# Where a softmax sum gets its small constant, and how many routing scatters a step issues

## The chip, the core and the metric

The kernel runs on one core of a Trainium2 chip. The metric is the device time of one launch in microseconds (us), taken as the median of a few runs. The core has five engines with a queue of instructions each: TensorE (PE in the profile, with PEld for its weight loads), VectorE (DVE), ScalarE (ACT), GpSimd (POOL) and SyncE (SP), which here only issues DMAs. An engine takes its instructions in the order in which they stand in its queue. Waits between engines go over semaphores.

## The reference

Three stages follow each other, all in float32. Only what matters here is shown.

```python
# attention: batch 4, heads 8, sequence 576, head size 64
scores = scale * (q @ k.T)
kth = the 32nd largest score of the row
attn = exp(where(scores >= kth, scores, -1e9) - max)
attn = attn / (sum(attn) + 1e-09)
x = attn @ v                       # 2304 tokens x 512
# dense expert
h = x @ w_in;  x = (h * clip(h + 3, 0, 6) / 6) @ w_out
# routed experts: 8 of them, the two best for each token
noisy = x @ w_gate + log1p(exp(x @ w_noise)) * noise
out[token] += weight * (relu(x[token] @ w1[e]) @ w2[e])
```

The change touches the sum with its `1e-09` and the writing of the routing lists.

## The kernel before, in words

**Attention and the dense expert** are one pipelined loop in `phase_a`. The 2304 tokens are 18 tiles of 128, each with 8 heads, so there are 144 pieces of (tile, head), and step `st` of the loop works on several pieces in different stages: transposes of `q` and `k` for one, scores for the one before, then the search for the 32nd largest score (two steps on VectorE), exponentials (ScalarE), the product `y` that finds the threshold (GpSimd, `ysum`), the mask with the row's sum (VectorE, `pmask`), the transposes of the masked row and the product with `v`. Two heads make a pair, and a pair's two sums stand in one small tile, `SUM[p]`. In the first step after a pair's second `pmask` its reciprocal is made in three moves: `recip1` adds 1e-9 on GpSimd, `recip2` takes the reciprocal on VectorE, `recip3` spreads it over 64 columns on GpSimd (`rb`), from where it goes to TensorE and then scales the pair's output.

In the same steps, once two tiles are through (a "chunk"), one of 16 slices of the dense expert is worked on per step: `mm1` (tile `h`), a gate on VectorE (`hgate`, tile `r`), rounding on ScalarE, the low part on GpSimd (`hlow`, tile `g`), `mm2` (tile `xa`).

From step 22 on (`KEEP`) the four engines get the loop's instructions in just the order in which the loop emits them; every call goes through the wrapper class `Lane` at line 87, so nearly all instructions of this phase carry L87 in the profile. Before step 22, and for routing, a planner that simulates the time places the instructions itself.

**Routing** is not part of that fixed order. When a chunk of the dense expert is done, `on_chunk` appends small pieces of work to the list `fill`, each with a weight, and every step takes pieces from the front of the list until a budget is used up: 4 (`NFILL`) per step as long as attention runs, 12 after step 148.

```python
room = NFILL if st < slots + OD else 3 * NFILL
while fill and room > 0:
    room -= fill[0][0]
    fill.pop(0)[1]()
```

A tile's logits are two pieces of weight 4; for each of four groups of tiles (6, 6, 4, 2) there are some 38 pieces of weight 1, three empty ones of weight 4 (`SCD`), and then two scatters for each tile of weight `SCW`. A scatter (L813) is an indirect DMA that GpSimd issues: it writes 128 pairs of (weight, token) to the lists `idw` in DRAM. A scatter is put behind the last `hlow` emitted so far (`pace`) and may otherwise move. With the loop's counts, the scatters of the first group (tiles 0 to 5) fall into steps 89 to 94, two in each, those of the second (6 to 11) into steps 137 to 142; the other two groups come when attention is over. Behind the scatters of the first group stand the logits of tiles 6 and 7 (steps 95 to 98), behind those of the second the logits of tiles 12 and 13 (143 to 146). An output tile of the dense expert (`xm`, two buffers) stays until its logits are made.

**The routed experts** (`phase_b`, from about 830 us) load the lists, gather tokens by indirect DMA, and do two matrix products per expert (`hb`, L935, and `ac`, L959). The first job needs all scatters of tiles 0 to 15.

The steps that matter for the change, in the order of the loop's body: `ysum` and `expo`; `recip1`; `mm1`; the transposes; on VectorE `ymax`, `recip2`, the search interleaved with the segments of the next piece, `hgate`, `zmask`, `pmask`; on GpSimd `recip3` and the rest; `mm2`; then what `fill` gives.

Of the kernel before, what the change touches and what calls it, by code (L numbers as in the profile page):

```python
# [7 lines left out]
F32 = mybir.dt.float32  # L8
# [5 lines left out]
ALU = mybir.AluOpType  # L14
# [162 lines left out]
def phase_a(tc, pools, ident, q, k, v, w_in, w_out, X, worst, wscr, stream, begin, on_chunk=None, slots=NSLOT, pace=None):  # L177
    nc = Lanes(tc)
    wp, ap, mp, ps, dr = pools
    TS, TT, STT = nc.vector.tensor_scalar, nc.vector.tensor_tensor, nc.vector.scalar_tensor_tensor  # L180
# [57 lines left out]
    def k_load(i):  # L238
        dl, b, h = ksched[i]
        KR[i] = kr = ap.tile([128, 5, 64], F32, name=f"kr{i}", tag="kr", bufs=KRB)  # L240
        nc.sync.dma_start(kr[:, 0:4, :], k[b, h, 0:512, :].rearrange("(p j) d -> p j d", j=4))
        nc.sync.dma_start(kr[0:64, 4, :], k[b, h, 512:576, :])
# [53 lines left out]
    def q_load(t, g):  # L296
        QR[t, g] = qr = ap.tile([128, 4, 64], F32, name=f"qr{t}_{g}", tag="qr", bufs=QRB)
        for (b, row, n, s0) in pieces(t):
            nc.sync.dma_start(qr[row:row + n], q[b, 4 * g:4 * g + 4, s0:s0 + n, :].rearrange("h s d -> s h d"))
# [24 lines left out]
    def scores(i):  # L324
        t, h = divmod(i, 8)
        p = ps.tile([128, 2, 512], F32, name=f"s{i}", tag="s")
        qts = QT.pop(i)
        for half in range(2):
            n = 2 * len(qts)
            m = 0  # L330
            for qt, (b, _, _, _) in zip(qts, pieces(t)):
                for j in range(2):
                    nc.tensor.matmul(p[:, half, 0:288], qt[:, j, :],
                                     KT[b, h][:, half * 288:(half + 1) * 288],
                                     start=(m == 0), stop=(m == n - 1))
                    m += 1
        PSS[i] = p

    def s_evac(i):
        p = PSS.pop(i)  # L340
        ss = ap.tile([128, 576], F32, name=f"ss{i}", tag="ss", bufs=SSB)
        nc.scalar.copy(ss.rearrange("p (a n) -> p a n", a=2), p[:, :, 0:288])
        SS[i] = ss
        ST[i] = ap.tile([128, NSEG, 8], F32, name=f"seg{i}", tag="seg", bufs=SEGB)
# [23 lines left out]
    def expo(i):  # L368
        if i % 2 == 0:
            EP[i // 2] = ap.tile([128, 1152], F32, name=f"e{i}", tag="e", bufs=EB)  # L370
        e = EP[i // 2][:, 576 * (i % 2):576 * (i % 2) + 576]
        E[i] = e
        nc.scalar.activation(e, SS[i], AF.Exp, bias=A8[i][:, 24:25], scale=0.125)
# [7 lines left out]
    def ysum(i):  # L381

        Y[i] = y = ap.tile([128, 584], F32, name=f"y{i}", tag="y", bufs=YB)
        nc.gpsimd.tensor_tensor(y[:, 0:576], Z.pop(i), SS[i], op=ALU.mult)

        nc.scalar.activation(y[:, 576:584], rank, AF.Relu, bias=fillc, scale=low[:, i:i + 1])
# [17 lines left out]
    SUM = {}  # L404

    def pmask(i):
        if i % 2 == 0:
            SUM[i // 2] = ap.tile([128, 2], F32, name=f"sum{i}", tag="sum", bufs=3)
        STT(E[i], SS.pop(i), T8[i // 8][:, i % 8, 7:8], E[i], op0=ALU.is_ge, op1=ALU.mult,
            accum_out=SUM[i // 2][:, i % 2:i % 2 + 1])  # L410

    def recip1(p):
        nc.gpsimd.tensor_scalar(SUM[p], SUM[p], 1e-9, 1.0, op0=ALU.add, op1=ALU.mult)

    def recip2(p):
        nc.vector.reciprocal(SUM[p], SUM[p])

    def recip3(p):
        r = SUM.pop(p)
        rb = ap.tile([128, 2, 64], F32, name=f"rb{p}", tag="rb", bufs=2)  # L420
        nc.gpsimd.tensor_scalar(rb, r[:, :, None].to_broadcast([128, 2, 64]), 1.0, 1.0, op0=ALU.mult, op1=ALU.mult)
        RB[p] = rb
# [69 lines left out]
    def w_fetch(u):  # L492
        c, fb = u
        if fb in stream:
            w = wp.tile([128, 2, 1024], F32R, name=f"ws{c}_{fb}", tag="ws", bufs=NSTR)
            nc.sync.dma_start(w.bitcast(F32), wscr[fb])
            W[u] = w
        else:
            W[u] = wres[fb]

    def mm1(u):
        c, fb = u
        n = 128 * len(chunks[c])
        w = W[u][:, :, 0:512].rearrange("p a (d f) -> p a d f", d=4)
        xt = XT[c]
        p = ps.tile([128, 512], F32, name=f"h{c}_{fb}", tag="h")
        m = 0
        for d in range(4):
            for a, b in ((0, 0), (0, 1), (1, 0)):
                o = nc.tensor.matmul(p[:, 0:n], w[:, a, d, :], xt[b][:, d, 0:n], start=(m == 0), stop=(m == 11))  # L510
                m += 1
        HP[u] = p
        lastmm[:] = [o]
# [14 lines left out]
    def hround(u):  # L528
        n = 128 * len(chunks[u[0]])
        g = mp.tile([128, 2, 256], F32R, name=f"g{u[0]}_{u[1]}", tag="g", bufs=GB)  # L530
        copy('g', g[:, 0, 0:n], R[u][:, 0:n])
        G[u] = g

    def hlow(u):
        n = 128 * len(chunks[u[0]])
        g = G[u]

        eng = nc.vector if ustep_of[u] > slots + OD else nc.gpsimd
        low = eng.tensor_tensor(g[:, 1, 0:n], R.pop(u)[:, 0:n], g.bitcast(F32)[:, 0, 0:n], op=ALU.subtract)
        if pace is not None:  # L540
            pace[:] = [low] if eng is nc.gpsimd else []
# [37 lines left out]
    ok = lambda i: 0 <= i < slots  # L579
# [4 lines left out]
    for st in range(-6, end):  # L584
        if st == -6: q_load(0, 0)
        if st == BEGIN: begin()
        if st == KEEP: nc.keep()
        if st % 4 == 0 and 0 < st // 4 + 1 < slots // 4: q_load(*divmod(st // 4 + 1, 2))
        for i, (dl, b, h) in enumerate(ksched):
            if max(dl - 4, min(i, 2) - 6) == st: k_load(i)  # L590
        for fb in wstep.get(st + 2, []): wk.load(fb)

        while fetched < len(units) and units[fetched][0] <= st + 3:
            w_fetch(units[fetched][1]); fetched += 1
        u, up = ustep.get(st), ustep.get(st - 1)
        s_, a, b, c, d, e, av_, x1, x2 = (st - x for x in (OS, OA, OB, OC, OD, OE, OV, OX, OY))
        ki = kdl.get(st)

        if up:
            hround(up)  # L600
            hlow(up)
        if ok(s_):
            scores(s_)
            s_evac(s_)
        if ok(c):
            ysum(c)
            expo(c)
        if ok(d - 1) and d % 2 == 0: recip1(d // 2 - 1)
        if u:
            mm1(u)  # L610
            hrelu(u)
        if ok(e):
            ptrans(e)
            ptevac(e)
        if ki is not None or ok(st):
            kq_trans(ki, st if ok(st) else None)
        if ok(st): q_evac(st)
        if ok(x1) and x1 % 2 == 0: xscale(x1 // 2)

        ch = chain(b) if ok(b) else []  # L620
        segs = [(a, j) for j in range(NSEG)] if ok(a) else []
        if ok(d): ymax(d)
        if ok(d - 1) and d % 2 == 0: recip2(d // 2 - 1)
        if ch:
            ch.pop(0)()
            nbias(b)
        while ch:
            if segs: seg(*segs.pop(0))
            ch.pop(0)()
        if segs: seg(*segs.pop(0))  # L630
        if u: hgate(u)
        if ok(b): zmask(b)
        if ok(d):
            pmask(d)
        while segs: seg(*segs.pop(0))

        if ok(d - 1) and d % 2 == 0: recip3(d // 2 - 1)
        if ok(x1) and x1 % 2 == 0: xscale2(x1 // 2)
        if up:
            mm2(up)  # L640
            if up[1] == NFB - 1: xout(up[0])
        if ki is not None:
            k_trans(ki)
            k_evac(ki)
        if ok(av_) and av_ % 2: av(av_ // 2)
        for i, (dl, b, h) in enumerate(ksched):
            if dl + VL == st: v_load(i)
        if ok(x2) and x2 % 2 == 0: xsplit(x2 // 2)
        if st % 4 == 2 and 0 <= st // 4 + 1 < slots // 4: q_split(*divmod(st // 4 + 1, 2))
        for i, (dl, b, h) in enumerate(ksched):  # L650
            if max(dl - 2, min(i, 2) - 5) == st: k_split(i)
        for fb in wstep.get(st, []): w_split(fb)
        for fb in wstep.get(st + 1, []): wk.convert(fb)
# [4 lines that stand above are left out]
# [10 lines left out]
EARLY = 1  # L668
DVE_JOBS = 4
NOID = 1 << 20  # L670
SCW = 2
SCD = 3
LTAG = "misc"
VG = 2
# [8 lines left out]
def make_route(tc, pools, ident, idw, w_gate, w_noise, noise, cnt, nt=NT, few=None, pace=()):  # L683
# [48 lines left out]
    def route(t0, n):  # L732
# [88 lines left out]
        if t0 + n == nt and nt == NT:  # L821

            def early():
# [5 lines left out]
        return ([(1, o) for o in ops] + [(NFILL, lambda: None)] * (SCD if t0 + n < nt else 1)  # L829
                + [(SCW, lambda j=j, z=z: scatter(j, z)) for j in range(n) for z in range(2)])  # L830

# [495 lines left out]
```

## Time and profile before

| | |
|---|---|
| median of 3 runs | 1393.41 us (1392.29 to 1394.97) |
| profiled execution | 1381.3 us, its span 1379.5 us |
| busy over the span: PE, DVE, ACT, POOL | 94%, 69%, 56%, 60% |
| chain that ended last | PE 37%, issue 3%, POOL 3%, DMA 2%, DVE 2%, ACT 1% of the span; it is followed back to 735 us |

Busy shares are averages over two very different phases: in attention (up to about 820 us) all engines work, later TensorE alone is busy most of the time. "Idle before" in a group of instructions is the time for which the engine had nothing to do just before them, and the name behind the arrow is what ended that time. A matmul's busy time counts its latency too, so a busy TensorE may still have room.

### The profile page before, as it was taken

The numbers are of one execution on the slowest core, as the hardware profiler recorded it, in microseconds if no ns is written. First come the engines' busy times: TensorE is split into PE (matmuls) and PEld (weight loads), VectorE is DVE, ScalarE is ACT, GpSimd is POOL, SyncE is SP. The second block draws the span as 40 slices with busy tenths as digits, with TensorE's granted clock in tenths as the row PEclk, the third lists the DMA queues.
The fourth block names the chain that finished last, engine by engine and source line by source line (L and its number), as shares of the span: only waits on it lengthen the run. The fifth ranks groups of instructions, "written<-read, shape, count | busy, mean of one in ns | idle before, by whom it ended". The sixth has DMA issues, their size and how long they took to land. (4 is left out here: it accounts for less than half of the span.)

```text
span 1379.5 us, 27084 instructions
## 1 busy us (share of the span) xinstructions
PE 1293.2 (94%) x9006; PEld 1121.2 (81%) x9006; DVE 948.3 (69%) x3560; ACT 770.2 (56%) x1709; POOL 829.9 (60%) x1159
## 2 busy tenths in 40 slices
PE   5878899999999989999999899899999999999996
PEld 3554689989888878898988688788988898898985
DVE  7999987899987978869989753446353545435241
ACT  6888777777778666777777554534322322222220
POOL 7666777677767786767687845133324547465451
PEclk9789999999999999999999999999999999999999
DMA  7776644545365353445544447846446556465431
GB/s 249 261 279 226 230 145 157 193 166 176 132 206 166 127 149 124 170 131 187 175 143 157 123 154 246 265 140 221 136 153 195 178 167 204 140 214 177 137 109 38
DMA packets 138100, 239.56 MB, mean 174 GB/s; under 512 B 39779, under 2 KB 93155, under 8 KB 123872
## 3 DMA queue, kind: packets, MB, share of 16 engines
q1 hardware_dynamic: 127600, 210.57, 46.1%
q0 software_dynamic: 10352, 27.18, 5.9%
q8 instruction: 73, 1.20, 0.4%
q14 instruction: 75, 0.61, 0.2%
HBM read 209.08 MB, written 31.64 MB: 174 GB/s over the span
## 5 line engine op out<-in xcount | busy, mean ns | idle before, releaser
L959 PE MATMUL ac<-w,hh 128*128 128x512 f32 x960 | 247.8, 400 | 1.6 <-ACT hh L941 1.5
L935 PE MATMUL hb<-xe,w 128*128 128x320 f32 (+2 forms) x1536 | 239.4, 311 | 1.0 <-DVE hh L942 0.5
L935 PEld LDWEIGHTS hb<-xe,w 128*128 128x128 f32 x1536 | 232.1, 189 | 10.0 <-issue 3.9
L87 DVE MAX8 seg<-ss 128x8 f32<-128x82 f32 (+1 forms) x1008 | 213.9, 231 | 4.1 <-ACT ss L87 3.7
L87 POOL TENSOR_TENSOR y<-z,ss 128x576 f32<-128x576 bf16 x144 | 205.3, 1426 | 11.7 <-DVE z L87 10.1
L941 ACT ACTIVATE hh<-hb 128x640 fp32r<-128x640 f32 (+2 forms) x72 | 46.6, 647 | 295.7 <-PE hb L935 295.7
L959 PEld LDWEIGHTS ac<-w,hh 128*128 128x128 f32 x960 | 172.8, 188 | 40.3 <-ACT hh L941 5.4
L942 DVE SCALAR_TENSOR_TENSOR hh<-hb,hh 128x640 fp32r<-128x640 f32 (+2 forms) x72 | 53.9, 749 | 213.2 <-ACT hh L941 213.2
L87 PE MATMUL h<-xT,ws 128*128 128x256 f32 x1188 | 159.1, 283 | 9.3 <-DVE r L87 7.9
L87 ACT COPY ss<-s 128x576 f32<-128x576 f32 x144 | 92.6, 643 | 134.6 <-DVE e L87 69.6
L87 PE MATMUL xa<-ws,g 128*128 128x512 f32 x594 | 163.9, 410 | 2.2 <-POOL g L87 0.9
L87 PEld LDWEIGHTS h<-xT,ws 128*128 128x128 f32 x1188 | 150.0, 190 | 12.8 <-DVE r L87 9.9
L921 POOL TENSOR_TENSOR w<-r,w 128x1024 fp32r<-128x1024 f32 x40 | 97.9, 2452 | 85.2 <-ACT w L919 73.4
L87 DVE SCALAR_TENSOR_TENSOR e<-ss,t,e 128x576 f32<-128x576 f32 x144 | 147.6, 1025 | 0.1
L87 POOL TENSOR_TENSOR g<-r,g 128x256 fp32r<-128x256 f32 x124 | 100.2, 808 | 39.8 <-issue 19.6
L87 PEld LDWEIGHTS xa<-ws,g 128*128 128x128 f32 x594 | 104.0, 190 | 23.6 <-POOL g L87 5.1
L87 DVE TENSOR_SCALAR_CACHE_REDUCE z<-ss,a 128x576 bf16<-128x576 f32 x144 | 115.8, 804 | 0.2
L87 ACT ACTIVATE e<-ss,a 128x576 f32<-128x576 f32 x144 | 110.6, 768 | 1.4 <-POOL a L87 1.4
L87 PE MATMUL s<-kt,qt 128*128 128x288 f32 x512 | 101.2, 321 | 7.8 <-ACT qt L87 6.8
L87 DVE MAX8 t<-y 128x8 f32<-128x584 f32 x144 | 107.8, 749 | 0.0
L975 POOL DMA_INDIRECT out_dram<-y,id x40 | 41.8, 1045 | 108.9 <-DVE y L974 86.7
L87 PE MATMUL pa<-ident,e 128*128 128x128 f32 x576 | 91.3, 283 | 15.4 <-DVE e L87 13.4
(427 smaller groups left out, 2617.2 us busy)
## 6 DMA issues: line engine op xcount, KB each, us to landing
ws<-wscr SPq DMA_DIRECT2D x99, 1024.0 KB, 4.8
r<-in_moe_w_dram SPq DMA_DIRECT2D x144, 256.0 KB, 3.1
wscr<-wsp SPq DMA_DIRECT2D x11, 1024.0 KB, 5.8
wraw<-in_moe_w_in_dram SPq DMA_DIRECT2D x16, 512.0 KB, 4.2
wraw<-in_moe_w_out_dram SPq DMA_DIRECT2D x16, 512.0 KB, 5.1
ck<-in_moe_w_in_dram SPq DMA_DIRECT2D x32, 256.0 KB, 3.4
ck<-in_moe_w_out_dram SPq DMA_DIRECT2D x32, 256.0 KB, 3.2
out_dram<-zero SPq DMA_DIRECT2D x18, 256.0 KB, 4.2
```

The lines of the kernel that those rows point to most:

```text
L87: o = f(*args, **kw)
L921: eng.tensor_tensor(w[:, 1], r, w.bitcast(F32)[:, 0], op=ALU.subtract)
L935: o = nc.tensor.matmul(p[:, half, 0:hn], w[:, a, d, :], XE[job][:, b, d, half * hn:(half + 1) * hn], start=(m == 0), stop=(m == 11))
L941: nc.scalar.activation(hv[:, 0], p[:, 0:nh, 0:hn], AF.Relu)
L942: LOW[:] = [STT(hv[:, 1], p[:, 0:nh, 0:hn], 0.0, h.bitcast(F32)[:, :, 0:n].rearrange("p a (b n) -> p a b n", b=nh)[:, 0], op0=ALU.max, op1 ...
L959: o = nc.tensor.matmul(ACC[job, j], h[:, a, j * 128:(j + 1) * 128], w[:, b, :], start=(x % NF2 == 0 and m == 0), stop=(x % NF2 == NF2 - 1 ...
L975: s = nc.gpsimd.indirect_dma_start(out=out, out_offset=bass.IndirectOffsetOnAxis(ap=t.bitcast(I32)[:, j, 1:2], axis=0), in_=y, in_offset=N ...
```

## The change

The addition of 1e-9 leaves GpSimd and goes to VectorE, just ahead of the reciprocal, as a `tensor_scalar` that also writes an accumulated sum to a third column which nobody reads. The weight of a scatter goes from 2 to 4, so a step of attention issues one scatter instead of two, and a step after attention three instead of six.

```diff
     def pmask(i):
         if i % 2 == 0:
-            SUM[i // 2] = ap.tile([128, 2], F32, name=f"sum{i}", tag="sum", bufs=3)
+            SUM[i // 2] = ap.tile([128, 3], F32, name=f"sum{i}", tag="sum", bufs=3)
         STT(E[i], SS.pop(i), T8[i // 8][:, i % 8, 7:8], E[i], op0=ALU.is_ge, op1=ALU.mult,
             accum_out=SUM[i // 2][:, i % 2:i % 2 + 1])
-    def recip1(p):
-        nc.gpsimd.tensor_scalar(SUM[p], SUM[p], 1e-9, 1.0, op0=ALU.add, op1=ALU.mult)
     def recip2(p):
-        nc.vector.reciprocal(SUM[p], SUM[p])
+        TS(SUM[p][:, 0:2], SUM[p][:, 0:2], 1e-9, None, op0=ALU.add, op1=ALU.add, accum_out=SUM[p][:, 2:3])
+        nc.vector.reciprocal(SUM[p][:, 0:2], SUM[p][:, 0:2])
     def recip3(p):
-        r = SUM.pop(p)
+        r = SUM.pop(p)[:, 0:2]
...
-        if ok(d - 1) and d % 2 == 0: recip1(d // 2 - 1)
...
-SCW = 2
+SCW = 4
```

With the new weight the scatters of the first group fall into steps 89 to 100 and the logits of tiles 6 and 7 into 101 to 104; those of the second group fall into steps 137 to 148, and the logits of tiles 12 and 13 into 149 and 150.

## Rows read from the trace of the kernel before

**Rows 1.** Busy time by stretch (us, each with its count); last row: TensorE alone.
```profile
core 0: us, PE busy (x) PEld busy (x) DVE busy (x) ACT busy (x) POOL busy (x), PEclk, DMA share, GB/s
0.00:100.00 100.00, 67.99 (x345) 45.72 (x346) 91.60 (x300) 78.66 (x160) 68.83 (x121) 0.85 0.77 260
...
300.00:400.00 100.00, 99.43 (x814) 89.19 (x813) 89.79 (x411) 74.29 (x188) 70.81 (x109) 1.00 0.49 165
...
1000.00:1100.00 100.00, 99.82 (x567) 89.29 (x566) 46.39 (x94) 27.14 (x35) 41.24 (x32) 1.00 0.54 175
...
484.00:534.00 50.00, 43.90 (x315) 0.90 0.51 146
```

**Rows 2.** Waits of DVE up to 820 us: total, times, longest.
```profile
DVE sum L87 <- POOL sum L87: 91.7, 63, 4.8
```

**Rows 3.** Chain that ended last: start us, us, what.
```profile
747.73 1.82 POOL y L87
...
749.64 0.20 POOL sum L87
...
770.99 1.35 POOL idw L813
```

**Rows 4.** Timeline of DVE, an ordinary pair: start us, us, operation, [idle before <- releaser].
```profile
308.40 0.17 DVE L87 RECIPROCAL sum<-sum 128x2 f32<-128x2 f32 x1 [0.48 <-POOL sum L87]
308.48 0.20 DVE L87 MAX8 a<-seg 128x8 f32<-128x56 f32 x1
...
317.99 0.17 DVE L87 RECIPROCAL sum<-sum 128x2 f32<-128x2 f32 x1 [0.48 <-POOL sum L87]
```

**Rows 5.** Timeline of DVE, the reciprocals around the two groups of scatters.
```profile
488.45 0.17 DVE L87 RECIPROCAL sum<-sum 128x2 f32<-128x2 f32 x1 [0.48 <-POOL sum L87]
501.89 0.17 DVE L87 RECIPROCAL sum<-sum 128x2 f32<-128x2 f32 x1 [4.79 <-POOL sum L87]
...
527.17 0.17 DVE L87 RECIPROCAL sum<-sum 128x2 f32<-128x2 f32 x1 [2.84 <-POOL sum L87]
537.15 0.17 DVE L87 RECIPROCAL sum<-sum 128x2 f32<-128x2 f32 x1 [0.48 <-POOL sum L87]
...
749.86 0.17 DVE L87 RECIPROCAL sum<-sum 128x2 f32<-128x2 f32 x1 [0.49 <-POOL sum L87]
...
797.88 0.17 DVE L87 RECIPROCAL sum<-sum 128x2 f32<-128x2 f32 x1 [0.49 <-POOL sum L87]
```

**Rows 6.** Timeline of POOL, one pair with four scatters.
```profile
505.27 1.37 POOL L813 DMA_INDIRECT idw<-pl,ix  x1 [0.15 <-issue]
...
507.93 1.31 POOL L87 TENSOR_TENSOR y<-z,ss 128x576 f32<-128x576 bf16 x1
...
514.29 0.19 POOL L87 TENSOR_SCALAR sum<-sum 128x2 f32<-128x2 f32 x1
514.88 0.19 POOL L87 TENSOR_SCALAR a<-a 128x1 f32<-128x1 f32 x1 [0.40 <-DVE a L87]
...
517.91 1.37 POOL L813 DMA_INDIRECT idw<-pl,ix  x1
```

**Rows 7.** Groups of instructions, whole span: count | busy us, mean ns | idle before.
```profile
L87 DVE TENSOR_SCALAR_CACHE_REDUCE z<-ss,a 128x576 bf16<-128x576 f32 x144 | 115.8, 804 | 0.2
...
L1048 DVE SCALAR_TENSOR_TENSOR cu<-cu 128x256 f32<-128x256 f32 x64 | 36.6, 590 | 0.8
...
L1048 DVE DVE_READ_ACCUMULATOR cu<-cu 128x1 f32 x64 | 5.2, 81 | 0.0
```

**Rows 8.** Chain that ended last, near the end of attention: TensorE's runs.
```profile
796.04 0.54 PE s L87 x4
...
813.37 1.50 PE av L87 x21
814.87 1.41 PE h L87 x12
816.28 0.44 PE pa L87 x4
...
816.82 1.38 PE xa L87 x6
```

## The prediction

> **What bounds the kernel now.** I read the stretches first. After 1000 us TensorE is busy 99.8% of the time and no other engine more than 46% [rows 1]; neither edit touches that phase, so what attention saves is kept to the end, and what it loses is lost. In attention the picture is mixed: from 300 to 400 us TensorE is busy 99.4% and VectorE 89.8%, while in the first 100 us VectorE leads with 91.6% and TensorE has 68% [rows 1]. Second, the waits of VectorE: one line stands far above the rest, 91.7 us of waiting for GpSimd's addition to the sums, 63 times [rows 2]. The kernel has 72 pairs, so all but 9 of them (the early ones) show it. Third, the chain that ended last, to see whether that wait is on the path: between 735 and 790 us it runs through GpSimd's `y`, then the addition, then VectorE, and through scatters [rows 3]. So the wait is real, but it must be asked pair by pair what stands behind it.
>
> An ordinary pair, from one reciprocal to the next, takes 317.99 - 308.40 = 9.59 us, and VectorE waits 0.48 us of it [rows 4]; its own work is 9.11. TensorE's work in a pair, by the runs where it alone sets the pace: one `av` run 1.50, and twice `h` 1.41, `pa` 0.44, `xa` 1.38, `s` 0.54, which makes 9.04 [rows 8], plus the transposes of `q` (two per step) and one of `pa`'s left over, five at most at 0.44/4 = 0.11 [rows 8], or 0.55. The sum is 9.59: in an ordinary pair TensorE has almost nothing to give. A short run may start inside the one before it, so I take the five transposes between 0.06 and 0.11 each and put TensorE's floor at 9.35 to 9.59.
>
> The pairs with scatters are another matter. From 488.45 the reciprocals lie 13.44 us apart, then 12.64 on the mean of two, then 9.98 [rows 5]: 48.70 us for four pairs where four ordinary ones take 38.36, so 10.3 too many. The second group has 797.88 - 749.86 = 48.02 us for four pairs [rows 5], 9.7 too many. Together **20.0 us are spent on two groups of 12 scatters**. The cause is in GpSimd's row: the period is 517.91 - 505.27 = 12.64 us, and two scatters with the gap between them take 507.93 - 505.27 = 2.66, so four take 5.32 [rows 6]. GpSimd is then the engine with too much to do. TensorE, starved, also gets a lower clock: 0.90 on the mean of 484 to 534 us, against 1.00 in the undisturbed stretch [rows 1].
>
> **The scatters, one a step.** Nothing is added or removed: the 24 scatters of attention are spread over 24 steps instead of 12, so 12 pairs carry two each. A pair's GpSimd period falls by 2.66 to 9.98, and without the addition (0.19 and the gap to the next instruction) by some 0.27 more, to 9.71; the 0.40 us for which GpSimd waits for VectorE's first maximum [rows 6] stood behind the reciprocal and may go too, to 9.31. That is at the level of TensorE's 9.59. Latencies will not fit perfectly, so I put such a pair at 9.6 to 10.3 and take 9.95. Twelve of them cost 12 x (9.95 - 9.59) = 4.3 us over ordinary ones where 20.0 were paid: **-15.7** (between -11.5 and -20.0). Each scatter still stands behind a `g`, and often ahead of a `y`; the next maximum needs that `y` only in the following step, so one scatter of 1.33 us ahead of it is hidden by VectorE's own 4 to 5 us of work in a step, while two, with the reciprocal waiting in the same step, were not. No transfer waits on this: the lists are not read before the routed experts. What is moved behind the scatters is logits. Those of tiles 6 and 7 go from steps 95 to 98 to steps 101 to 104, still one step ahead of the next output tiles (step 105), which need their buffers; the same work lies in other steps, 0 us. Those of tiles 12 and 13 fall into two steps after attention, three pieces in one of them, where TensorE works alone; it can lose up to one `h` run (1.41 [rows 8]) in each, nothing if the planner interleaves. I take **+1.0**.
>
> **The addition on VectorE.** Added on VectorE: one reducing `tensor_scalar` on two columns and the read of its accumulator, 72 times; removed: 72 additions on GpSimd and the wait. No row has this size. From below: the reciprocal on the same two columns lets the next instruction start 0.08 us later [rows 4], so 0.08. From above: a 256-column operation with accumulator, 0.59 and 0.08 [rows 7], so 0.67; the 576-column one of the same form, at 0.80 [rows 7], is farther off. I take 0.20: two instructions at the reciprocal's 0.08, and a little because each needs the result of the one before. VectorE queues the whole search of the step behind it, and the reciprocal's reader (`rb`, then the pair's output) is steps away from being late.
>
> What it does depends on the pair. In the 9 early pairs no wait is there to be removed and VectorE leads: 9 x 0.20 = **+1.8** (0.7 to 6.0). In an ordinary pair VectorE's need becomes 9.11 + 0.20 = 9.31, below TensorE's floor, so the 0.48 us of wait go and TensorE is late next. The gain is what TensorE has in hand, 0 to 0.24; I take 0.10. There are 63 - 6 = 57 waiting pairs without scatters, 6 of which get scatters now, which leaves 51: **-5.1** (0 to -12). That most of the 91.7 us is not gained is the point: where a wait is longest among these pairs (tiles that span two batches, routing), TensorE has more matmuls in the step.
>
> [...]
>
> **Sum.** -15.7 + 1.0 + 1.8 - 5.1 = -18.0 us against the profiled execution's 1381.3 us, of which 1379.5 are its span. The median shown is 1393.4, 12 us above that execution; I carry the difference over unchanged: 1393.4 - 18.0 = **1375.4**.
>
> **Rivals.**
> *A step with a scatter stalls whatever their number.* If what costs is that GpSimd's queue is interrupted once (the order `g`, scatter, `y`, or the wait of a scatter's start), and not the 1.33 us of each, then 12 steps at 20.0/12 = 1.67 us become 24: +20.0, less 5.1 and plus 2.8, so 1411. It decides at 0.83 us per step with one scatter; above that the change loses on the scatters. For it: the scatters stand ahead of `y`, on which VectorE's order hangs. Against: VectorE's wait in such a pair (2.84) is at the reciprocal [rows 5], and that wait is cut. **0.12**.
> *Nothing comes of it.* Either the planner, which may move scatters, puts them together again, so that the 20.0 us stay and 1393.4 - 5.1 + 1.8 = 1390 is left, or the new VectorE work costs 0.67: 9 x 0.67 = 6.0 early and 51 x (0.67 - 0.48) = 9.7 later, so -15.7 + 1.0 + 15.7 = +1.0, or 1394. For it: VectorE is over 89% busy in attention. Against: a pair with scatters is short of GpSimd time, not of VectorE time. **0.11**.
> *All of the wait is gained that VectorE can give.* TensorE's floor is lower than its runs say, and an ordinary pair falls to VectorE's 9.31: 51 x 0.28 = 14.3; the scatters cost nothing more, 20.0; with 1.8 for the early pairs, -32.5: 1361. Against it: TensorE's 99.4%. **0.09**.
> The forecast has **0.68**, with its own range from 1365 to 1387 (the terms' ends, without adding them all on one side).
>
> **How the numbers follow.** A measurement of this kernel tells changes from about 0.2%, 2.8 us, so "same" is 1390.6 to 1396.2. Faster: the forecast and the large gain, 0.77, with a little of the second rival's 1390; same 0.10; slower: the first rival and a mishap in the planner's order before step 22, 0.13. The range runs from 1361, the large gain, to 1391, with the slow side left out.
>
> **What would show it.** Right: reciprocals some 10 us apart throughout the scatters, over twice as many pairs, GpSimd's groups showing one scatter between two `y`; the clock at 1.00 there; VectorE's wait for `sum` gone, with ordinary pairs still at 9.3 to 9.6; an added VectorE group of about 0.2 us busy. Wrong: pairs with two scatters over 11.3 us; VectorE idle before `t` (the maximum of `y`) instead; ordinary pairs longer than 9.6; or early reciprocals several us later than before.

## The result, and the profile after

The changed kernel takes **1374.88 us** (median of 4 runs, 1372.91 to 1378.40) where the kernel before, on the same chip, takes 1394.19 us (4 runs, 1392.29 to 1396.26). The ratio is 0.9864, with a 95% interval from 0.9837 to 0.9891: 19 us faster. Its profiled execution takes 1373.47 us, of which 1371.6 are the span.

Three stretches by engine, and TensorE alone where the first group of scatters was (columns as in [rows 1]):

```profile
0.00:100.00 100.00, 70.37 (x344) 45.57 (x344) 88.40 (x301) 76.95 (x156) 66.33 (x114) 0.86 0.78 261
300.00:400.00 100.00, 99.52 (x816) 89.39 (x815) 91.15 (x438) 73.94 (x188) 67.35 (x99) 1.00 0.47 159
1000.00:1100.00 100.00, 98.44 (x557) 87.55 (x556) 45.85 (x93) 29.38 (x38) 50.96 (x38) 1.00 0.56 180
...
484.00:534.00 50.00, 50.00 (x410) 1.00 0.52 167
```

The last row is the change in short: from 484 to 534 us TensorE is busy 50.00 us of 50 at a granted 1.00, where it was busy 43.90 us at a granted 0.90 [rows 1]. From 300 to 400 us nothing that matters moved: TensorE was busy 99.43 us of 100 [rows 1] and is busy 99.52.

The largest wait of VectorE up to 820 us. The wait for GpSimd's sum [rows 2] is gone, and another, for the scores that ScalarE copies (`ss`), has taken its place:

```profile
DVE seg L87 <- ACT ss L87: 60.5, 66, 2.6
```

The reciprocals, in the timeline of VectorE; first three ordinary pairs, then the two stretches of scatters:

```profile
308.87 0.13 DVE L87 TENSOR_SCALAR_CACHE_REDUCE sum<-sum 128x2 f32<-128x2 f32 x1
308.93 0.08 DVE L87 DVE_READ_ACCUMULATOR sum<-sum 128x1 f32 x1
309.05 0.17 DVE L87 RECIPROCAL sum<-sum 128x2 f32<-128x2 f32 x1
...
318.13 0.17 DVE L87 RECIPROCAL sum<-sum 128x2 f32<-128x2 f32 x1
...
327.66 0.17 DVE L87 RECIPROCAL sum<-sum 128x2 f32<-128x2 f32 x1
...
338.74 0.17 DVE L87 RECIPROCAL sum<-sum 128x2 f32<-128x2 f32 x1
...
488.53 0.17 DVE L87 RECIPROCAL sum<-sum 128x2 f32<-128x2 f32 x1
...
525.66 0.17 DVE L87 RECIPROCAL sum<-sum 128x2 f32<-128x2 f32 x1
...
737.29 0.17 DVE L87 RECIPROCAL sum<-sum 128x2 f32<-128x2 f32 x1
...
774.91 0.17 DVE L87 RECIPROCAL sum<-sum 128x2 f32<-128x2 f32 x1
```

The added pair of instructions starts 309.05 - 308.87 = 0.18 us ahead of the reciprocal. The four pairs that took 48.70 and 48.02 us [rows 5] take 525.66 - 488.53 = 37.13 and 774.91 - 737.29 = 37.62 us: 9.28 and 9.40 each. GpSimd there, with one scatter between two `y` where there were two [rows 6]:

```profile
504.84 1.04 POOL L811 DMA_INDIRECT idw<-pl,ix  x1 [0.16 <-issue]
...
506.06 0.74 POOL L87 TENSOR_TENSOR g<-r,g 128x256 fp32r<-128x256 f32 x1
506.97 1.04 POOL L811 DMA_INDIRECT idw<-pl,ix  x1 [0.17 <-issue]
508.04 1.31 POOL L87 TENSOR_TENSOR y<-z,ss 128x576 f32<-128x576 bf16 x1
...
513.67 1.04 POOL L811 DMA_INDIRECT idw<-pl,ix  x1
...
514.89 1.36 POOL L87 TENSOR_TENSOR g<-r,g 128x256 fp32r<-128x256 f32 x1
```

### The profile page after: what moved, and what is told of

It is laid out like the page before. It is cut to its first block, busy times and chain, and to the rows that moved or that the text cites. A ratio compares the mean times of both kernels' runs of the same rounds, so it can differ in the third digit from the quotient of the medians.

```text
span 1371.6 us, 27163 instructions
## 1 busy us (share of the span) xinstructions
PE 1289.7 (94%) x9006; PEld 1120.8 (82%) x9006; DVE 941.6 (69%) x3704; ACT 768.9 (56%) x1709; POOL 814.7 (59%) x1087
## 3 DMA queue, kind: packets, MB, share of 16 engines
q1 hardware_dynamic: 127600, 210.57, 46.4%
q0 software_dynamic: 10352, 27.18, 6.1%
## 4 chain that ended last, share of the span: by engine, by line
PE 70%; DVE 4%; issue 4%; ACT 3%; POOL 2%; DMA 1%; POOLq 0%; ACTq 0%; SPq 0%
PE ac L957 16%; PE hb L933 16%; PE xa L87 11%; PE h L87 10%; PE av L87 6%; PE s L87 4%; PE pa L87 3%; PE et L897 1%; DVE seg L87 1%; POOL idw L811 1%; DVE e L87 1%; PE lg L727 1%; PE qpNone L87 1%; DVE z L87 1%; DMA idw<-pl,ix 1%
## 5 line engine op out<-in xcount | busy, mean ns | idle before, releaser
L87 DVE MAX8 seg<-ss 128x8 f32<-128x82 f32 (+1 forms) x1008 | 215.0, 233 | 60.9 <-ACT ss L87 60.5
L87 POOL TENSOR_TENSOR y<-z,ss 128x576 f32<-128x576 bf16 x144 | 200.3, 1391 | 14.9 <-DVE z L87 13.3
L87 DVE SCALAR_TENSOR_TENSOR e<-ss,t,e 128x576 f32<-128x576 f32 x144 | 139.3, 967 | 0.1
L87 POOL TENSOR_TENSOR xs<-xs 128x128 f32<-128x128 f32 x72 | 53.7, 745 | 116.4 <-ACT xs L87 115.2
```

The lines of the kernel that those rows point to most:

```text
L87: o = f(*args, **kw)
```

## The experiments

Twelve runs, in four groups, each group on a chip of its own, and each ratio is to the kernel before on that chip. One table holds what the traces say; all its times are starts read from the timelines (the reciprocals of the 72 pairs on VectorE, numbered from 0 as in the profile's order; the scatters on GpSimd; the `hb` matmuls of the routed experts on TensorE, of which the first job has 96, so that the 97th is the first of the second job). "Ordinary" is the mean pair from reciprocal 12 to 38, "scatters" the mean of the four pairs from reciprocal 41 and of the four from 65.

| kernel | ratio, 95% interval | ordinary, us | scatters, us | reciprocal 71 at | first `hb` to last four scatters | first to 97th `hb` |
|---|---|---|---|---|---|---|
| before | 1 | 10.63 | 12.18, 12.00 | 814.2 | 11.5 | 39.5 |
| before_again | 0.9996 [0.9983, 1.0009] | 10.63 | 12.20, 12.01 | 815.7 | 11.7 | 39.7 |
| before_third | 1.0012 [0.9986, 1.0038] | 10.63 | 12.18, 12.01 | 814.0 | 11.1 | 40.5 |
| only_scw | 0.9945 [0.9927, 0.9964] | 10.63 | 11.15, 11.14 | 809.6 | 11.3 | 40.7 |
| only_add | 0.9935 [0.9916, 0.9954] | 10.62 | 10.92, 10.76 | 800.5 | 18.3 | 48.2 |
| after | 0.9864 [0.9837, 0.9891] | 10.61 | 9.28, 9.40 | 791.3 | 15.9 | 43.0 |
| after_again | 0.9856 [0.9820, 0.9892] | 10.61 | 9.28, 9.40 | 790.5 | 18.3 | 47.7 |
| after_third | 0.9891 [0.9847, 0.9934] | 10.62 | 9.28, 9.40 | 790.6 | 15.8 | 46.4 |
| scw1 | 0.9984 [0.9956, 1.0011] | 10.61 | 11.92, 11.84 | 809.3 | 18.3 | 48.1 |
| add_early | 0.9876 [0.9839, 0.9914] | 10.59 | 10.01, 9.79 | 794.6 | 16.0 | 45.9 |
| add_twice | 0.9897 [0.9871, 0.9923] | 10.61 | 9.57, 9.55 | 800.3 | 12.1 | 39.9 |
| no_add | 0.9805 [0.9786, 0.9823] | 10.61 | 9.29, 9.40 | 788.7 | 12.3 | 40.1 |
| no_add_again | 0.9833 [0.9794, 0.9872] | 10.61 | 9.29, 9.40 | 787.9 | 12.3 | 38.0 |
| route_first | 0.9823 [0.9783, 0.9863] | 10.61 | 9.28, 9.40 | 789.9 | 12.0 | 41.2 |

Within attention the three traces of one kernel agree at reciprocal 71 within 0.8 us (the changed kernel) and 1.7 us (the kernel before), which is finer than the timed intervals, so the attention's part is read from them.

**Four together: each half of the change, the change without the addition, and the kernel before again.** Against the kernel before, and for no_add against the changed one:

```diff
only_scw, in the kernel before
-SCW = 2
+SCW = 4
only_add, in the changed kernel
-SCW = 4
+SCW = 2
no_add, in the changed kernel
-        TS(SUM[p][:, 0:2], SUM[p][:, 0:2], 1e-9, None, op0=ALU.add, op1=ALU.add, accum_out=SUM[p][:, 2:3])
```

Expected of before_again:

> The kernel before, unchanged, for a second profile: the first profiled execution took 1381.3 us where the timed ones took 1392 to 1396. Theory: attention repeats itself (reciprocals 12.6 us apart with four scatters in a pair) and the 12 us lie in the routed experts, which in the profile before went from the first hb at 891 us to the last at 1361 (470 us) and in the changed kernel took 481. Rival: the 12 us lie in attention, and the routed experts take 470 us again.

Expected of only_scw:

> One scatter a step; the addition stays on GpSimd. Theory (GpSimd's time per pair decides): the four pairs' excess of 10 us falls to 4 us or less per group, spread over twice as many pairs; time 12 to 14 us below before, about 1381. Rival (a step with a scatter stalls whatever their number): no better than before, 1394 to 1410. Second rival (the wait at the reciprocal is what costs): no change, 1394.

Expected of only_add:

> The addition on VectorE; two scatters a step as before. Theory: pairs with four scatters stay at 12.4 us since GpSimd has as much to do; ordinary pairs lose 0.1 to 0.2 us; 4 to 6 us below before, about 1389. Rival (the wait at the reciprocal is what costs in the scatter pairs): these fall to about 11 us or less and the time to 1380.

Expected of no_add:

> The changed kernel without the addition of 1e-9 (left out altogether; the reciprocal is taken of the plain sum). Theory: VectorE's added 0.2 us count only in the 9 early pairs, so 1 to 3 us below the changed kernel. Rival (VectorE leads everywhere): 72 x 0.2 = 14 us below it.

Measured: 0.9945 for the scatters alone (-7.6 us), 0.9935 for the addition alone (-9.0), where I had expected most from the scatters. At reciprocal 71, against the mean 814.6 of the three traces of before, they are 5.0 and 14.1 us early, the whole change (mean of its three, 790.8) 23.8, more than the two together. So the theory that GpSimd's load alone makes the long pairs falls: only_scw missed its 12 to 14 us, and of only_add the rival came true, with pairs under 11 us. Of its 14.1 us only_add keeps 9.0 in the time; its start of the routed experts is slow (48.2 us to the 97th `hb`, before_again 39.7), on which more below. no_add ends attention 2.5 us ahead of the changed kernel (means of two and three traces), far from the rival's 14, but by the two ratios, from different chips, it is some 8 us faster, more than its theory's 1 to 3; the rest lies in the start of the routed experts. before_again repeats the first profile: attention ends 1.5 us later, and from the first `hb` to the last it takes 470.2 us as against 470.0, so it does not show where the 12 us between that profile and the median lie.

With the scatters spread but the addition still on GpSimd, VectorE's reciprocals lie 11.1 us apart and wait in every pair:

```profile
511.24 0.17 DVE L87 RECIPROCAL sum<-sum 128x2 f32<-128x2 f32 x1 [1.58 <-POOL sum L87]
522.32 0.17 DVE L87 RECIPROCAL sum<-sum 128x2 f32<-128x2 f32 x1 [1.58 <-POOL sum L87]
```

and GpSimd's queue shows what for:

```profile
508.21 1.37 POOL L813 DMA_INDIRECT idw<-pl,ix  x1 [0.16 <-issue]
509.62 1.31 POOL L87 TENSOR_TENSOR y<-z,ss 128x576 f32<-128x576 bf16 x1
511.01 0.19 POOL L87 TENSOR_SCALAR sum<-sum 128x2 f32<-128x2 f32 x1
511.60 0.19 POOL L87 TENSOR_SCALAR a<-a 128x1 f32<-128x1 f32 x1 [0.40 <-DVE a L87]
```

One scatter and one `y`, 2.8 us, still stand ahead of the addition; VectorE, whose next maximum stands behind the reciprocal, stops for it, and GpSimd stops 0.40 us in return for that maximum (`a`). With the addition on VectorE and two scatters a step this loop is cut, but GpSimd's own row is long (busy 27.18 of the 30 us from 494 to 524): four scatters of 0.96 to 1.36 us and their gaps in a pair, and the next pair starts 10.7 us later. Spreading these scatters, all that the changed kernel adds, takes such pairs from 10.92 and 10.76 to 9.28 and 9.40.

```profile
505.41 1.36 POOL L811 DMA_INDIRECT idw<-pl,ix  x1 [0.16 <-issue]
507.07 0.97 POOL L811 DMA_INDIRECT idw<-pl,ix  x1 [0.30 <-issue]
...
509.13 1.04 POOL L811 DMA_INDIRECT idw<-pl,ix  x1 [0.17 <-issue]
510.48 0.96 POOL L811 DMA_INDIRECT idw<-pl,ix  x1 [0.30 <-issue]
...
516.12 1.60 POOL L811 DMA_INDIRECT idw<-pl,ix  x1 [0.16 <-issue]
```

**A second chip: the change again, the addition twice, the addition early, four scatters a step.**

```diff
add_twice, in the changed kernel, behind the addition
+        TS(SUM[p][:, 0:2], SUM[p][:, 0:2], 0.0, None, op0=ALU.add, op1=ALU.add, accum_out=SUM[p][:, 2:3])
add_early, in the kernel before, with SCW = 4: GpSimd adds ahead of its y
+        if ok(d - 1) and d % 2 == 0: recip1(d // 2 - 1)
         if ok(c):
             ysum(c)
             expo(c)
-        if ok(d - 1) and d % 2 == 0: recip1(d // 2 - 1)
scw1, in the changed kernel
-SCW = 4
+SCW = 1
```

Expected of after_again:

> The changed kernel, unchanged, for a second profile. In the first, attention ended 22 us earlier than before but the routed experts took 481.5 us (first to last hb) instead of 470, in part behind starts of ScalarE that nothing in the trace explains. Theory (it belongs to this program): the second profile has 478 to 483 us again. Rival (an accident of one execution): 470 to 474, and attention as in the first profile.

Expected of add_twice:

> The changed kernel with the addition followed by a second one of 0.0 in the same form, so 0.18 us more of VectorE in each of 72 pairs. Theory (in ordinary pairs TensorE leads and VectorE has room): attention ends 1 to 3 us later than in the changed kernel, from the early pairs. Rival (VectorE leads): 72 x 0.18 = 13 us later.

Expected of add_early:

> One scatter a step; the addition stays on GpSimd but is issued ahead of y instead of behind it, so that VectorE need not wait for y. Theory (the gain is the cut wait, not the engine): attention ends where it does in the changed kernel or 1 to 3 us earlier, 20 to 25 us before the kernel before. Rival (the addition must leave GpSimd's full queue): no better than one scatter alone, 6 us before the kernel before.

Expected of scw1:

> The changed kernel with four scatters a step, so three steps per group. Theory (each scatter costs its GpSimd time once the step is full): worse than two a step with the same addition, whose two groups lost about 7 us each against one a step; 9 to 12 us per group here, attention 18 to 24 us longer than in the changed kernel. Rival (a step with scatters stalls whatever their number): half the steps of two a step, 3 to 4 us per group, attention 6 to 8 us longer.

Measured: after_again repeats attention (790.5 us at reciprocal 71), but takes 491.6 us from the first `hb` to the last, more than its theory (478 to 483) and its rival (470 to 474) allowed; the last section comes back to that. add_early leaves the addition on GpSimd and takes only the `y` (and the scatter ahead of it) out of its way. VectorE's waits for the sum fall from 88.1 us in only_scw to 37.6; 794.6 at reciprocal 71 is 3.8 us behind the changed kernel (level with it, or 1 to 3 us ahead, was expected), and 15.0 ahead of only_scw. So most of the gain is that of the cut wait, and does not need another engine for the addition; the rival, no better than only_scw, is out. scw1 puts the long pairs back (11.9 us) and is 18.5 us behind the changed kernel, within the 18 to 24 expected: a price per scatter, against the rival of one stall per step (6 to 8).

add_twice missed its expectation: 9.5 us behind at reciprocal 71, where I had expected 1 to 3 and the rival 13. The table says where. Over 26 ordinary pairs the second addition costs nothing (10.61). It costs 5.5 us ahead of reciprocal 12 (188.3 against 182.8), where VectorE leads, and the other 4 us from reciprocal 38 on: 2.1 in the three pairs ahead of each group of scatters (38 to 41 and 62 to 65), 1.5 in the two stretches with scatters, 0.5 between them. The six pairs follow VectorE's work: they take 60.3 us in the kernel before, 58.3 in the changed kernel, 57.4 in no_add and 60.5 in add_twice. In the stretches with scatters the mask on VectorE changed its own length. The group of masks from 488 to 554 us, in the kernel before, then in the changed kernel, add_twice and no_add:

```profile
L87 DVE SCALAR_TENSOR_TENSOR e<-ss,t,e 128x576 f32<-128x576 f32 x11 | 12.1, 1103 | 0.0
```

```profile
L87 DVE SCALAR_TENSOR_TENSOR e<-ss,t,e 128x576 f32<-128x576 f32 x14 | 13.0, 926 | 0.0
```

```profile
L87 DVE SCALAR_TENSOR_TENSOR e<-ss,t,e 128x576 f32<-128x576 f32 x14 | 17.2, 1225 | 0.0
```

```profile
L87 DVE SCALAR_TENSOR_TENSOR e<-ss,t,e 128x576 f32<-128x576 f32 x14 | 12.5, 892 | 0.0
```

The same mask takes 0.89 to 1.23 us on the mean. Over the whole of these four traces, a mask beside which GpSimd has nothing to do takes 0.79 to 0.82 us (14 or 15 in each), and one that overlaps a `g` 1.12 to 1.17 us on the mean. In the window above, 8 of 11, 3 of 14, 9 of 14 and 3 of 14 masks overlap a `g`, in the order of the four lines, which goes with their means. In the changed kernel, two of them:

```profile
510.01 0.81 DVE L87 SCALAR_TENSOR_TENSOR e<-ss,t,e 128x576 f32<-128x576 f32 x1
...
514.23 1.30 DVE L87 SCALAR_TENSOR_TENSOR e<-ss,t,e 128x576 f32<-128x576 f32 x1
```

The second runs beside GpSimd's `g` at 514.89, which takes 1.36 us there and 0.74 at 506.06 (above). So both are longer in this overlap; what lengthens them is not shown. That a shift of 0.18 us brings more masks into that overlap is read from these counts, and was not tried by itself.

**A third chip: the kernel before, the changed one and no_add once more**, for the profiles of the routed experts.

Expected of before_third:

> The kernel before on the same chip as the two next. ScalarE's unexplained late starts in the routed experts showed in all profiles of one chip so far and in none of another, whatever the kernel. Theory (they belong to the chip): this profile has them if and only if the two next have; from first to last hb 470 us without them, 480 to 490 with them. Rival (they belong to programs with the addition on VectorE): none here, some in the changed kernel beside it.

Expected of after_third:

> The changed kernel beside the kernel before. Attention 21 to 24 us shorter, the run-out of the dense expert 1 to 2 us longer. Theory (the rest of the difference is the planner's order at the start of the routed experts): the last four scatters 4 to 6 us later after the first hb than in the kernel before, and the experts 3 to 8 us longer; 16 to 20 us faster in all. Rival: on one chip the experts take the same time, 21 us or more faster in all.

Expected of no_add_again:

> The changed kernel without the addition, beside it. As before: attention 1.5 to 3 us shorter, the last four scatters as early as in the kernel before, the experts 3 to 8 us shorter than in the changed kernel; 5 to 10 us faster than it, 26 to 28 faster than the kernel before. Rival (its lead was that of a quiet chip): no more than 3 us faster than the changed kernel.

Measured: 1.0012, 0.9891 and 0.9833. Attention ends where it did in each kernel's earlier traces, so its gain is the same on the chips profiled. From the first `hb` to the last the three take 480.7, 492.7 and 485.7 us, where before_third's theory has 480 to 490 with late starts of ScalarE. From 890 us on ScalarE idles ahead of a slice (`hh`) for no releaser 5 times in before_third, 25.5 us in all, and 3 times in after_third, 11.6 us. after_third's scatters come 4.7 us later than in before_third, as expected, but its experts take 12.0 us longer where 3 to 8 were expected, and it is 15 us faster in all, a little less than its 16 to 20. no_add_again is 9 us faster than the changed kernel beside it, as expected, and 23 us faster than the kernel before, less than the 26 to 28. The first part of the routed experts does differ by kernel (last two columns of the table). On GpSimd, before_third, the first of the last four scatters:

```profile
903.45 1.02 POOL L813 DMA_INDIRECT idw<-pl,ix  x1 [25.55 <-DVE ix L805]
```

The same in after_third:

```profile
886.04 1.02 POOL L811 DMA_INDIRECT idw<-pl,ix  x1 [29.66 <-DVE ix L803]
```

Their first `hb` matmuls stand at 892.3 and 870.3 us, so the scatters come 11.1 us behind it before and 15.8 after. TensorE, waiting for the gathered rows, in before_third and in after_third:

```profile
920.34 0.66 PE L899 MATMUL et<-ident,xg 128*128 128x128 f32 x4 [2.13 <-DMA xg<-X,id]
```

```profile
903.53 1.12 PE L897 MATMUL et<-ident,xg 128*128 128x128 f32 x4 [7.12 <-DMA xg<-X,id]
```

The reason is in VectorE's order, after_third: an expert slice (`hh`) that waits for ScalarE stands inside the chain of the last routing group (`rt` to `ix`), and two more follow before `ix`.

```profile
873.77 0.17 DVE L753 TENSOR_TENSOR rt<-rt 128x16 f32<-128x16 f32 x1
874.47 0.56 DVE L940 SCALAR_TENSOR_TENSOR hh<-hb,hh 128x384 fp32r<-128x384 f32 x1 [0.53 <-ACT hh L939]
...
878.80 0.56 DVE L940 SCALAR_TENSOR_TENSOR hh<-hb,hh 128x384 fp32r<-128x384 f32 x1 [0.81 <-ACT hh L939]
...
883.23 0.56 DVE L940 SCALAR_TENSOR_TENSOR hh<-hb,hh 128x384 fp32r<-128x384 f32 x1 [0.68 <-ACT hh L939]
...
885.66 0.16 DVE L803 CAST ix<-rs 128x2 int32<-128x2 f32 x1
```

Before, `hh` at 897.04 and 900.60 stand ahead of `ix` at 903.08: two, and neither waits. This place is ordered by the planner, and no edit touches it by hand; that other instructions in attention make it choose otherwise is inferred. It falls either way with small edits: in the table the scatters come 11.1 to 12.3 us behind the first `hb` in seven traces (add_twice among them; route_first, below, is not counted) and 15.8 to 18.3 in six, and the 97th `hb` comes after 38.0 to 40.7 us in those seven and 43.0 to 48.2 in those six.

**The last run takes that order back.** The changed kernel with three order dependencies (VectorE's first `hh` behind the last group's X1 and the second behind its `oh`, TensorE's third `hb` behind its last `po`), no work added or left out:

```diff
-        add(lambda: V.reduce_max(X1, b0, axis=AX.X))
+        add(lambda: MARK.update(x1=V.reduce_max(X1, b0, axis=AX.X)))
...
+                    m += 1; after(tc, o, MARK["po"]) if g == 2 and m == 1 and half == 0 else None
...
+                      op0=ALU.max, op1=ALU.subtract)]; after(tc, LOW[0], MARK[("x1", "oh")[g]]) if g < 2 else None
```

`MARK` remembers an instruction (`oh` and `po` are noted likewise, not shown); `after` sets the order.

Expected of route_first:

> The changed kernel with three order dependencies at the start of the routed experts and nothing else: VectorE's first two expert slices (hh) stand behind the last routing group's X1 and oh, and TensorE's third slice (hb) behind that group's po, so that the engines take them in the order that the kernel before has there. Theory (in the changed kernel the order of VectorE at the start of the routed experts, in which two hh stand inside the last group's chain, delays the last four scatters and with them the second job's rows): the last four scatters start 11 to 13 us after the first hb (the changed kernel: 15.8 to 18.3; the one before: 11 to 13), TensorE's wait for the first rows of the second job falls from 7 us to under 3, and the stretch from the first hb to the 96th is 4 to 7 us shorter than in the changed kernel's profiles, so the time is 0.3% to 0.5% below the changed kernel's, ratio to before 0.982 to 0.985. Rival (the late scatters only accompany another cause, such as the experts starting earlier against transfers that do not): the scatters come early, but the wait for the rows or another wait of the same length stays, and the ratio is that of the changed kernel, 0.986 to 0.989. Attention is the same in both (its end at 785 to 787 us).

Measured: 0.9823 [0.9783, 0.9863]. GpSimd, VectorE and TensorE, in the three views of the same places:

```profile
883.53 1.03 POOL L811 DMA_INDIRECT idw<-pl,ix  x1 [27.55 <-DVE ix L803]
```

```profile
876.50 0.55 DVE L940 SCALAR_TENSOR_TENSOR hh<-hb,hh 128x384 fp32r<-128x384 f32 x1
...
880.64 0.56 DVE L940 SCALAR_TENSOR_TENSOR hh<-hb,hh 128x384 fp32r<-128x384 f32 x1 [1.33 <-ACT hh L939]
...
883.09 0.16 DVE L802 CAST ix<-rs 128x2 int32<-128x2 f32 x1
```

```profile
900.42 1.11 PE L897 MATMUL et<-ident,xg 128*128 128x128 f32 x4 [2.15 <-DMA xg<-X,id]
```

The scatters come 12.0 us behind the first `hb` (871.6), TensorE waits 2.15 us where it waited 7.12, and the 97th `hb` comes 41.2 us behind the first, where it came after 43.0 to 47.7. So the order is the cause of the late scatters and of that wait, on one trace of this kernel. The first `hb` itself is 0.5 to 1.3 us later than in the changed kernel's traces, so at the 97th `hb`, 912.8 us against 914.1, 916.7 and 918.2, 1.3 to 5.4 us are left. The ratio lies within the theory's range, but its interval reaches the changed kernel's ratios, and the two were not timed on one chip: how much of a median it is worth stays at that.

## Why the prediction was right, and where it was not

The time came out as forecast (1374.9 against 1375.4), but by terms that missed on both sides: the scatters gave 7 us more than their term, ordinary pairs 3.6 us less, and 5.8 us were lost where nothing was forecast. That these nearly cancel is luck. Means of the three traces of each kernel:

| step of the prediction | predicted, us | measured, us | from |
|---|---|---|---|
| early pairs, to reciprocal 12 | +1.8 | +0.3 | 182.42 to 182.76 |
| ordinary pairs, 12 to 41 and 54 to 65 | -5.1 | -1.5 | 306.8 to 305.3; 111.8 to 111.9 |
| scatters, 41 to 54 and 65 to 71 | -15.7 | -22.7 | 149.2 to 136.9; 64.3 to 54.0 |
| after attention, 71 to first `hb` | +1.0 | +1.5 | 78.3 to 79.8 |
| start of the routed experts | none | +5.8 | 39.9 to 45.7 |
| sum | -18.0 | -16.5 | 932.9 to 916.3 at the 97th `hb`; timed: 19, 20 and 15 by the three ratios |

**The addition's price** was right: 0.18 us against 0.20 taken, and 26 ordinary pairs do not pay it. What it costs in the early pairs is not resolved: the kernel before's three traces differ by 1.6 us at reciprocal 12, more than the +0.3 of the row.

**Ordinary pairs.** The mechanism held: TensorE is late next. From 300 to 400 us its matmuls wait 0.4 us in all in the changed kernel. (The prediction had 51 such pairs; the row holds 40, the other 11 are among those of the next row.) That VectorE's work does not set the length is shown from both sides, since a pair has 10.61 us with no addition, with one and with two, and 10.63 with the wait; that TensorE's does is read from its row, as no run changes its work. What was off is the size: of the row's 1.5 us, 1.1 come from the three pairs ahead of the first scatters, where VectorE leads (above), and 0.4 from the 26 others; from 54 to 65 three such pairs gain 0.8 and the rest lose 0.9. I took 0.10 us for each of 51 pairs, from one pair of 9.59 us [rows 4]. Such pairs did shrink, to 318.13 - 309.05 = 9.08 and 9.53 us, but the next one, in which TensorE also makes the routing's logits of a tile (as it does there in the kernel before), grew to 338.74 - 327.66 = 11.08. The logits' rows in the changed kernel (`lt`, `lg`):

```profile
328.14 0.60 PE L716 MATMUL lt<-ident,xm 128*128 128x128 f32 x4
...
332.10 0.96 PE L727 MATMUL lg<-wgn,lx 128*128 128x16 f32 x8
```

In the kernel before the third of these pairs ended here:

```profile
337.72 0.17 DVE L87 RECIPROCAL sum<-sum 128x2 f32<-128x2 f32 x1 [0.49 <-POOL sum L87]
```

Three pairs took 337.72 - 308.40 = 29.32 us there and 338.74 - 309.05 = 29.69 after: VectorE ran ahead and then waited for `ss`. Over the chunk's eight pairs (reciprocal 24 to 32) the kernel before takes 79.0 us and the changed one 79.3. One pair was too small a sample; the price stands on a whole chunk.

**The scatters.** This is the step that failed: "The cause is in GpSimd's row", so that the pair falls "by 2.66 to 9.98" when two scatters leave it, and the addition gives "some 0.27 more". Spread alone, the pair came to 11.15, not 9.98; the addition alone gave 1.3 us a pair (12.18 to 10.92), not 0.27. Both together, 2.9, exceed the sum of the two, 2.3 (over the whole stretches of the row: 22.7 against 4.6 and 12.6), because either obstacle keeps the other's gain: GpSimd's load, and the loop in which VectorE waits for the addition behind scatter and `y` and GpSimd then for VectorE. I had the second as a remark (the reciprocal waits in the same step) and priced the first. The size was off too: -22.7 lies beyond the end of the term, -20.0, since such a pair fell below an ordinary one of before, to 9.28 and 9.40 against 9.59. TensorE was busy 50.00 of 50.00 us there, so its own need in such a pair is no more than that, where the forecast's floor was 9.35 to 9.59; an estimate for the twelve pairs is 12 x (9.59 - 9.34) = 3.0 us, about what the end of the term was exceeded by. Shorter masks can have a part in it, 2 x (1.103 - 0.926) = 0.35 us of VectorE a pair; the two were not told apart.

**What was not forecast** is the start of the routed experts. I had looked for the planner only ahead of step 22; it also sets the border between routing and experts, and a gain of 5.8 us went there. route_first shows the cause of most of it: with the order taken back, 41.2 us to the 97th `hb` instead of 45.7 on the mean, where the kernel before has 39.9.

The rivals: a stall per step is out (scw1). "Nothing comes of it" is out. "All of the wait is gained" was right on the scatters and wrong on ordinary pairs. The addition itself could go, by the reference's arithmetic: in float32 a row's sum, which holds the maximum's exp(0) = 1, does not change when 1e-9 is added. Without the instruction (no_add) the ratio is 0.9805 and 0.9833, level with route_first's 0.9823 within the intervals. Of its advantage over the changed kernel, 790.8 - 788.3 = 2.5 us stand at the end of attention and 45.7 - 39.1 = 6.6 in the start of the routed experts (means of its two traces), where its order is that of before.

## What to carry to other kernels

When two engines wait for each other in a loop, price the load and the wait together: here removing either alone brought 5.0 and 14.1 us of attention, and both together 23.8. Take a stretch's price from a whole period of the work (here all the pairs of a chunk, those with logits and those without), not from its most regular pair. And after an edit to one phase compare the order of the instructions at the next border that a planner arranges: here it took back 5.8 of those 23.8 us without a line of it being changed.

## What the runs showed that I had not expected

The kernel before took 1381.3 us in its profiled execution and, by chip, 1387 to 1399 in the median. The traces show where such a difference can lie: in the routed experts ScalarE sometimes starts a slice long after TensorE has delivered it. Its waits from 890 us on, in before_third and then in the first profile of the kernel before:

```profile
ACT hh L941 <- PE hb L935: 250.0, 63, 6.5
...
ACT hh L941 <- issue: 25.5, 5, 9.1
```

```profile
ACT hh L941 <- PE hb L935: 295.7, 72, 6.5
```

One such start, in before_third's timeline: ScalarE idles 9.10 us for no releaser, the last 4.4 of them after the slice's matmuls have ended (977.6 us), and TensorE then waits 3.54 us for it.

```profile
981.96 0.70 ACT L941 ACTIVATE hh<-hb 128x640 fp32r<-128x640 f32 x1 [9.10 <-issue]
982.72 1.62 PE L959 MATMUL ac<-w,hh 128*128 128x512 f32 x3 [3.54 <-ACT hh L941]
```

From the 97th `hb` to the last takes 430.4 to 430.5 us in five profiles (the first of the kernel before and the first group's four) and 438 to 452 in the other nine. The kernel before has 430.5 on one chip and 440.3 on another, no_add 430.4 and 447.7. So the kernel before can be slow there, and no_add, which has all of the change but the addition, need not be: it goes with the chip, or with the run. The changed kernel itself has 438.5, 443.9 and 446.3 in its three profiles, none of them with the first group, so that the change adds nothing to this stretch is not shown. What causes it stays open.
